# A gated mix of a long convolution and attention: x transposed half by the crossbar and half by TensorE, and another threshold for zero matmuls

## The chip, the cores and the metric

One Trainium2 chip, of which the program uses one core. A core has TensorE (matmuls, in the profile PE, its weight loads PEld), VectorE (DVE), ScalarE (ACT), GpSimd (POOL) and SyncE (SP), each working through its own list of instructions in order, and 16 DMA engines. The engines meet at semaphores. The metric is the device time of one execution in microseconds; times named here are medians of several runs, unless a profiled execution is meant.

## The reference

Two branches read the same x = A_q of shape 1 x 2048 x 640. One is a convolution: k is filtered with four taps, multiplied by v, convolved over the whole sequence with a long filter, and multiplied by x. The other is attention with 32 query heads of 20 channels that share one key head and one value head. A gate, the sigmoid of a dot product of x with gate_w, mixes them.

```python
def _B_ref(x, wq, wk, wv, wo):
    q = (x @ wq).reshape(B, S, H, Dh).transpose(0, 2, 1, 3)
    k = x @ wk
    v = x @ wv
    scores = einsum("bhqd,bkd->bhqk", q, k) * (Dh ** -0.5)
    p = softmax(scores, axis=-1)
    o = einsum("bhqk,bkd->bhqd", p, v)
    return o.transpose(0, 2, 1, 3).reshape(B, S, H * Dh) @ wo

x = A_q
g = sigmoid((x * gate_w).sum(-1, keepdims=True))
a = _A_ref(x, A_k, A_v, A_shift_k, A_ssm_k, A_ssm_D)   # q * (conv(kv, ssm_k) + kv * ssm_D)
b = _B_ref(x, B_wq, B_wk, B_wv, B_wo)
return g * a + (1 - g) * b
```

The scores of attention are 32 x 2048 x 2048, and every one of them is exponentiated. In the kernel that is the work of ScalarE (most of it) and VectorE.

## The kernel before

The kernel is written as a graph of operations, each with an engine, the operations it depends on, a rough cost and a priority. A planner (class Scheduler) then walks a clock over the five engines. On each engine it takes, of the operations that are ready by its own estimates, the one with the lowest priority number, and so fixes the order of every engine's list before the program is built. Waits on semaphores are put in from the dependencies (emit). So an edit of a priority or of an estimated latency moves instructions, and a wait stands wherever an instruction needs what another engine or a DMA made.

Two kinds of TensorE work are not in the graph. Where the planner finds nothing to do and TensorE's planned busy share over the last 2.4 us is under FILL, it puts in a matmul of zeros: in the opening from filler0 (L1486), during the stream of exponentials from filler (L1482), there only if the next score group is more than 0.1 us away.

**The opening** (up to the first exponential). x has four blocks of 512 rows, b = 0 to 3. Attention needs x transposed, xT, with channels on partitions. Blocks 0 to 2 come by DMA transpose through the crossbar, issued from SP (L722). Block 3 is loaded as it is into xn (L565) and transposed by TensorE in three groups of 8, 8 and 4 (L865), each copied from PSUM into xT by ScalarE or VectorE (copy_alts, L598 and L599; the planner picks). From xT come: kvn, one group of 20 small matmuls a block, giving k, v and the gate's dot product by rows (L907); kT, k transposed and repeated for four row groups (L893); and qp, the q projection of the first two of eight groups of heads (L949). The gate's weights reach the matmul operand wkv by one small transpose (L885) and one copy (L887), and kvn waits for it.

A bound on the scores is folded into the queries: ScalarE squares k out of kvn's PSUM bank (ksq, L913), VectorE sums (ksum, L920) and takes the maximum (kmcol, L923), a matmul spreads it (L926), three small operations make a root of it (kmaxr, kroot), and with the root of the squared queries (sq L959, q2 L965, ci L971) one operation makes the row cr (L974). A DMA from SP writes it into qT (the list crow0 holds this DMA). The first score matmuls (L1023) wait for that DMA. Many things that belong to later stages are made to wait for crow0 as well: loads of k, v and the remaining blocks of xn (load_x, which the convolution needs), second halves of the trigonometric tables on POOL (tables2), and the rest of wq.

ScalarE also makes the first part of the sine and cosine tables (L791, L794), with the Sin activation table; then an activation named warm (L798) loads the Exp table, after all the Sin operations.

**The stream.** attention() lists 767 exponentials of alternately 3 and 2 score tiles of 128 x 512 (ETA in banks 0 to 2, ETB in banks 3 and 4; L1055). Score group n+1 may start when exponential n-1 has freed its banks. DVE_J names the tiles that VectorE exponentiates with integer operations instead. Matmuls of probabilities with v (L1097) accumulate in bank 6. The convolution's spectra, products and inverse, later q projections and output projections are fitted around these by the planner, in banks 5 and 7. After the last exponential a short tail (tail) finishes the last group of heads, with TensorE, VectorE and the output DMAs.

The edit touches loads, tables, xT, load_x, kproj, qproj and the constants FILL and NX.

Of the kernel before, what the change touches and what calls it, by code (L numbers as in the profile page):

```python
# [18 lines left out]
FILL = 0.55  # L19
# [494 lines left out]
MAC_ALT = ()  # L514
SCALE = float(DH) ** -0.5
# [14 lines left out]
def c_act(n):  # L530
    return 0.18 + 0.833e-3 * n
# [10 lines left out]
class Kernel:  # L542
# [162 lines left out]
    def loads(self):  # L705
        T, aps = self.T, self.aps
        x = aps["A_q"][0].rearrange("(i p) d -> p i d", p=128)
        self.dma(T["wkv"][:, :, 0:20], aps["B_wk"].rearrange("(dc p) c -> p dc c", p=128), writes=["wk"],
                 nbytes=50000, eng="act", prio=-98.8)
        self.dma(T["wkv"][:, :, 20:40], aps["B_wv"].rearrange("(dc p) c -> p dc c", p=128), writes=["wv"],  # L710
                 nbytes=50000, eng="act", prio=-98.7)
        wq = aps["B_wq"].rearrange("(dc p) n -> p dc n", p=128)
        self.dma(T["gw5"][:, :], aps["gate_w"].rearrange("(dc p) -> dc p", p=128), writes=["gw5"], nbytes=2000,
                 eng="act", prio=-98.65)
        self.dma(T["wqst"][:, :, 0:160], wq[:, :, 0:160], writes=[("wqst", 0)], nbytes=204800, eng="act", prio=-98.6)
        xl = None
        x = aps["A_q"][0].rearrange("(i p) d -> p i d", p=128)
        self.dma(T["xn"][:, 12:16, :], x[:, 12:16, :], writes=[("xn", 3)], nbytes=655360, prio=-9)
        for b in range(NB - 1):
            o = T["xT"][:, :, 512 * b:512 * b + 512]  # L720
            i = aps["A_q"][0][512 * b:512 * b + 512, :]
            xl = self.g.add("sp", lambda e, o=o, i=i: e.dma_start_transpose(o, i), (), [("xT", b)], 0.1, kind="d",  # L722
                            nbytes=655360, prio=-8 + b, lat=1.6)
            xl.iss = 3.3

        self.xl = [xl]
        self.dma(T["wqst"][:, :, 160:640], wq[:, :, 160:640], writes=[("wqst", 1)], nbytes=614400, prio=-4,
                 after=self.xl)
        self.dma(T["Dbc"][:, :], aps["A_ssm_D"].partition_broadcast(128), writes=["Dbc"], nbytes=163840, prio=30,
                 after=self.xl)  # L730
# [39 lines left out]
    def tables(self):  # L770
# [6 lines left out]
        for c in range(H):  # L777
# [21 lines left out]
                            ["warm"], 1.5, prio=-1500.0, after=list(sins)))  # L799
        self.sins = sins  # L800
# [55 lines left out]
    def xT(self):  # L856

        T = self.T
        b = NB - 1
        for d0, nd in ((0, 2), (2, 2), (4, 1)):  # L860
            gr = self.group("xT", 1.0, banks=(0, 1, 2, 3, 4, 5, 7))
            for dc in range(d0, d0 + nd):
                for ci in range(4):
                    i = 4 * b + ci
                    self.mm(gr, lambda e, bk, i=i, dc=dc, ci=ci, d0=d0: e.transpose(  # L865
                        self.bank_bf(bk, 128, 512 * (dc - d0) + 128 * ci), T["xn"][:, i, 128 * dc:128 * dc + 128],
                        T["ident"][:, :]), [("xn", b), "ident"], 0.09)
            out = T["xT"][:, d0:d0 + nd, 512 * b:512 * b + 512]
            al = self.copy_alts(out, lambda bk, nd=nd: self.bank_bf(bk, 512 * nd).rearrange(
                "p (d t) -> p d t", d=nd), True)  # L870
            self.evac(gr, "dve", None, (), [("xT", b)], 0.45, alts=al)

    def load_x(self):
        T = self.T
        x = self.aps["A_q"][0].rearrange("(i p) d -> p i d", p=128)
        for b in range(NB - 1):
            self.dma(T["xn"][:, 4 * b:4 * b + 4, :], x[:, 4 * b:4 * b + 4, :], writes=[("xn", b)], nbytes=655360,
                     prio=30 + b, name="ld_x", after=self.crow0)

    def kproj(self):  # L880
# [8 lines left out]
        for b in range(NB):  # L889
            gr = self.group("kT", (1.16 if b == 0 else 4.0) + 0.1 * b, banks=ALLB if b == 0 else (7, 4, 5))  # L890
# [11 lines left out]
        for b in range(NB):  # L902
            gr = self.group("kvn", 1.5 + 0.1 * b, banks=ALLB)
            for ci in range(4):
                tc = 4 * b + ci
                for dc in range(NDC):
                    self.mm(gr, lambda e, bk, ci=ci, tc=tc, dc=dc: e.matmul(  # L907
                        self.bank(bk, 41, 44 * ci), T["xT"][:, dc, 128 * tc:128 * tc + 128], T["wkv"][:, dc, 0:41],
                        start=(dc == 0), stop=(dc == NDC - 1)), [("xT", b), "wk", "wv", "wg"], 0.05)

            def view(bk, lo, n=20):
                return self.bank(bk, 176).rearrange("p (t c) -> p t c", c=44)[:, :, lo:lo + n]
            self.evac(gr, "act", lambda e, bk, b=b, view=view: e.activation(  # L913
                T["ksq"][:, 4 * b:4 * b + 4, :], view(bk, 0), ACT.Square), (), [("ksq", b)], c_act(80))
# [7 lines left out]
                     name="ksum")  # L922
        self.dve(lambda e: e.tensor_reduce(T["kmcol"][:, :], T["ksum"][:, :], AX.X, ALU.max),  # L923
# [17 lines left out]
    def qproj(self, I, gs, prio, banks, ng):  # L941
# [3 lines left out]
        par = I % 2  # L945
        for gl, gi in enumerate(gs):
            gr = self.group("qp", prio, banks=banks)
            for dc in range(NDC):
# [4 lines left out]
                if dc == 0:  # L953
# [4 lines left out]
                      alts=self.copy_alts(qt[:, gi, :], lambda bk: self.bank(bk)))  # L958
            self.dve(lambda e, gi=gi, gl=gl: e.tensor_tensor(T[f"sq{gl}"][:, :], qt[:, gi, :], qt[:, gi, :],  # L959
                                                             ALU.mult),  # L960
                     [("qT", par, gi)], [("sq", gl)], c_fast(512), prio=prio - 500, port=True, name="sq")
        gr = self.group("q2", prio - 500, banks=banks)
# [7 lines left out]
        pr = -5000.0 if I == 0 and gs[0] == 0 else prio - 500  # L970
# [570 lines left out]
```

## Time and profile before

| | |
|---|---|
| median of five runs | 908.62 us (907.76 to 909.42) |
| profiled execution, its time | 908.86 us |
| profiled execution, its span | 906.8 us |
| first exponential starts | 23.65 us |
| last exponential ends | 897.44 us |
| ETA, 128 x 1536, one | 1489 ns mean, 384 of them |
| ETB, 128 x 1024, one | 1072 ns mean, 383 of them |
| zero matmuls, opening and stream | 18 and 149 weight loads |

The span is what the profile's clock covers from the first to the last instruction; a run's own time is some 2 us longer. Durations of exponentials overlap, since ScalarE starts one while the last drains, so the sum of the two means over all is more than the engine's busy time; the chain of waits counts each only from where the one before it ended. In the page's rows "idle before" is the time in which the engine stood still just ahead of such an instruction, with what ended most of it.

### The profile page before, as it was taken

Reading aid. Unit: us, or ns where it says so; the run is one execution under the profiler, and the core shown is the slowest. Engines: PE = TensorE matmul, PEld = TensorE weight load, DVE = VectorE, ACT = ScalarE, POOL = GpSimd, SP = SyncE. Lnnn points to the kernel's source line nnn. Section 1 sums busy time; section 2 is a strip of 40 time slices with the busy share of each in tenths; the row PEclk is TensorE's granted clock in tenths of the full one; section 3 lists DMA queues with packets and bytes.
Section 4 is the critical chain, followed back from the end, with each engine's and each line's share of the span. In section 5 each row is a group of like instructions: output and inputs, shape, how many; then the busy total and the mean of one; then the engine's idle time right before and its main releaser. Section 6 shows DMA issues by size and latency. Waiting matters only on the chain.

```text
span 906.8 us, 16333 instructions
## 1 busy us (share of the span) xinstructions
PE 852.0 (94%) x6950; PEld 350.4 (39%) x7013; DVE 633.0 (70%) x878; ACT 884.2 (98%) x791; POOL 380.5 (42%) x330
## 2 busy tenths in 40 slices
PE   7999999999999999999999999999999998998897
PEld 3344344443433344343333333343443332432233
DVE  6456743456766768866886678876678886787964
ACT  5999999999999999999999999999999999999995
POOL 2940056870426496153675212769125494000000
PEclk9999999999999999999999999999999999999999
DMA  7930200010000010000010200000000000301111
GB/s 163 212 128 3 65 20 20 13 31 18 20 19 14 15 35 20 19 20 17 14 32 18 56 20 13 19 8 19 20 19 19 14 7 26 89 13 35 63 35 52
DMA packets 58507, 32.69 MB, mean 36 GB/s; under 512 B 41154, under 2 KB 54466, under 8 KB 58434
## 3 DMA queue, kind: packets, MB, share of 16 engines
q1 hardware_dynamic: 56168, 31.05, 12.7%
q8 instruction: 55, 0.90, 0.4%
q10 hardware_dynamic: 2266, 0.59, 0.3%
q14 instruction: 18, 0.15, 0.1%
HBM read 18.01 MB, written 6.02 MB: 27 GB/s over the span
## 4 chain that ended last, share of the span: by engine, by line
ACT 68%; PE 24%; DMA 3%; SPq 2%; DVE 2%; issue 1%; DVEq 0%
ACT ETA L1055 41%; ACT ETB L1055 27%; PE ps L1023 7%; PE ps L1336 5%; PE ps L1097 5%; PE ps L1400 3%; PE ps L949 2%; SPq L1253 1%; DMA rbc<-scr_d 1%; DMA kTr<-in_A_k_dram 1%; DMA xT<-in_A_q_dram 1%; PE ps L1270 1%; PE ps L1434 1%; PE ps L1187 1%; SPq L722 1%
## 5 line engine op out<-in xcount | busy, mean ns | idle before, releaser
L1055 ACT ACTIVATE ETA<-ps 128x1536 bf16<-128x1536 f32 x384 | 571.7, 1489 | 3.6 <-PE ps L1097 2.3
L1055 ACT ACTIVATE ETB<-ps 128x1024 bf16<-128x1024 f32 x383 | 410.7, 1072 | 0.2 <-PE ps L1023 0.2
L1023 PE MATMUL ps<-qT,kT 21*128 21x512 bf16 x2048 | 302.5, 384 | 34.8 <-ACT ETA L1055 22.8
L1367 POOL TENSOR_TENSOR Pp<-X,K 128x512 f32<-128x512 bf16 x120 | 168.6, 1430 | 358.4 <-DVE K L1355 351.0
L1097 PE MATMUL ps<-ETA,vaug 128*32 128x512 bf16 x1150 | 196.1, 389 | 0.4 <-DVE acc L1151 0.3
L1097 PE MATMUL ps<-ETB,vaug 128*32 128x512 bf16 x766 | 188.1, 389 | 0.0
L1023 PEld LDWEIGHTS ps<-qT,kT 21*128 21x128 bf16 x2048 | 74.7, 91 | 223.6 <-ACT ETA L1055 123.2
L1085 DVE TENSOR_SCALAR dJ<-ps 128x512 uint32<-128x512 f32 x132 | 90.7, 687 | 44.0 <-PE ps L1023 43.7
L1093 DVE SCALAR_TENSOR_TENSOR ETd<-dJ,dE 128x1024 bf16<-128x1024 f32 x66 | 89.4, 1354 | 19.5 <-PE ps L1097 19.4
L1090 DVE SCALAR_TENSOR_TENSOR dE<-dJ,dE 128x1024 f32<-128x1024 uint16 x66 | 89.9, 1362 | 0.5
L1092 DVE SCALAR_TENSOR_TENSOR dJ<-dJ 128x1024 f32<-128x1024 uint16 x66 | 89.3, 1353 | 0.4
L1367 POOL TENSOR_TENSOR AB<-Pp 128x256 bf16<-128x256 f32 x80 | 77.2, 965 | 4.9
L1400 PE MATMUL ps<-AB,Tcos 128*128 128x256 bf16 x320 | 78.2, 275 | 1.1 <-DVE dJ L1085 1.0
L1097 PEld LDWEIGHTS ps<-ETA,vaug 128*32 128x32 bf16 x1150 | 47.7, 93 | 65.6 <-issue 63.0
L1400 PE MATMUL ps<-AB,Tsin 128*128 128x256 bf16 x280 | 69.3, 275 | 0.0
L1097 PEld LDWEIGHTS ps<-ETB,vaug 128*32 128x32 bf16 x766 | 45.2, 92 | 43.5 <-issue 42.9
L1367 POOL TENSOR_TENSOR Pp<-Pp 128x512 f32<-128x512 f32 x40 | 60.9, 1524 | 2.7
L1088 DVE TENSOR_SCALAR dE<-dJ 128x1024 uint32<-128x1024 uint32 x66 | 54.1, 820 | 0.5
L1336 PE MATMUL ps<-ssm_kT,Tsin 128*128 128x256 bf16 x320 | 53.7, 275 | 0.0
L1336 PE MATMUL ps<-kv,Tsin 128*128 128x256 bf16 x320 | 53.7, 275 | 0.0
L1336 PE MATMUL ps<-kv,Tcos 128*128 128x256 bf16 x320 | 52.0, 275 | 1.2 <-DVE kv L1410 0.5
L1336 PE MATMUL ps<-ssm_kT,Tcos 128*128 128x256 bf16 x320 | 51.8, 275 | 0.4 <-DVE dJ L1085 0.3
(135 smaller groups left out, 807.2 us busy)
## 6 DMA issues: line engine op xcount, KB each, us to landing
rbc<-scr_d SPq DMA_DIRECT2D x31, 256.0 KB
scr_o<-oTn SPq DMA_DIRECT2D x24, 128.0 KB, 1.7
xn<-in_A_q_dram SPq DMA_DIRECT2D x4, 640.0 KB
kv<-in_A_v_dram SPq DMA_DIRECT2D x4, 640.0 KB, 5.1
out_dram<-outsb SPq DMA_DIRECT2D x14, 160.0 KB, 1.8
oTp<-scr_o SPq DMA_DIRECT2D x12, 160.0 KB, 5.2
wog<-in_B_wo_dram SPq DMA_DIRECT2D x4, 200.0 KB
wo<-in_B_wo_dram SPq DMA_DIRECT2D x4, 200.0 KB, 3.4
```

Source lines behind the costliest of these rows:

```text
L949: o = self.mm(gr, lambda e, bk, gi=gi, dc=dc: e.matmul(self.bank(bk), T["wq_pad"][:, dc, 128 * gi:128 * gi + 128], T["xT"][:, dc, 512 * I: ...
L1023: return e.matmul(self.bank(bk), T["kT4"][32 * r:32 * r + 21, 128 * j:128 * j + 128], T[f"qT{G // 8 % 2}"][32 * r:32 * r + 21, G % 8, :], ...
L1055: op("act", lambda e: e.activation(et(n)[:, 0:w], self.ps[:, lo:lo + w], ACT.Exp, scale=SCALE), [("ps", base[n % 2] + k) for k in range(le ...
L1085: self.evac(gr, "dve", lambda e, bk, h=h: e.tensor_scalar(J[:, 512 * h:512 * h + 512], self.bank(bk), SCALE * LOG2E * 65536.0, EOFF * 6553 ...
L1088: V(lambda e: e.tensor_scalar(E[:, :], J[:, :], 7, 0x7F800000, ALU.logical_shift_left, ALU.bitwise_and), [kJ], ["dE"], c_fast(1024), **k)
L1090: V(lambda e: e.scalar_tensor_tensor(Ef, lo, ED, Ef, ALU.add, ALU.mult), [kJ, "dE"], ["dE"], c_ps(1024), **k)
L1092: V(lambda e: e.scalar_tensor_tensor(Jf, lo, EP, lo, ALU.add, ALU.mult), [kJ], [kJ], c_ps(1024), **k)
L1093: V(lambda e: e.scalar_tensor_tensor(T["ETd"][:, :], Jf, EQ, Ef, ALU.add, ALU.mult), [kJ, "dE"], ["ETd"], c_ps(1024), **k)
L1097: return op("pe", lambda e: e.matmul(self.bank(6)[32 * r:32 * r + 32, :], T["vaug"][:, j, :], src, start=(j == 0), stop=(j == NSC - 1), ti ...
L1336: o = self.mm(gr, lambda e, bk, lhs=lhs, rhs=rhs, comp=comp, n=n: e.matmul(self.bank(bk, 256, 256 * comp), lhs, rhs, start=(n == 0), stop= ...
L1367: f = lambda e: e.tensor_tensor(out, a, b, alu)
L1400: self.mm(gr, lambda e, bk, lhs=lhs, fc=fc, comp=comp, h=h: e.matmul(self.bank(bk, 256, 256 * h), lhs, AB[:, fc, :, comp, :], start=(fc == ...
```

## The change

Five things are edited.

- **x.** NX = 2: blocks 0 and 1 come by crossbar transposes, blocks 2 and 3 are loaded into xn and transposed by TensorE, so 40 transposes in six groups instead of 20 in three. The copies out of PSUM get a high priority. load_x, after crow0, brings two blocks of xn instead of three.
- **Gate weights.** Their load moves to the head of ScalarE's DMA queue, with a longer estimated latency.
- **kT of block 0** gets a later priority (1.95 instead of 1.16), behind the kvn groups of lower number.
- **Squares and the bound.** ksq, the first q copies, their squares and q2 get high priorities, and the activation that loads the Exp table now depends on all four ksq.
- **FILL** goes from 0.55 to 0.62.

```diff
-FILL = 0.55
+FILL = 0.62
...
+NX = 2
...
         self.dma(T["gw5"][:, :], aps["gate_w"].rearrange("(dc p) -> dc p", p=128), writes=["gw5"], nbytes=2000,
-                 eng="act", prio=-98.65)
+                 eng="act", prio=-98.9, lat=6.2)
...
-        self.dma(T["xn"][:, 12:16, :], x[:, 12:16, :], writes=[("xn", 3)], nbytes=655360, prio=-9)
-        for b in range(NB - 1):
+        for b in range(NX, NB):
+            self.dma(T["xn"][:, 4 * b:4 * b + 4, :], x[:, 4 * b:4 * b + 4, :], writes=[("xn", b)], nbytes=655360,
+                     prio=-9)
+        for b in range(NX):
             o = T["xT"][:, :, 512 * b:512 * b + 512]
...
-            xl.iss = 3.3
+            xl.iss = 4.8 if b == 0 else 3.3
...
+        self.warm = sins[-1]
...
-        b = NB - 1
-        for d0, nd in ((0, 2), (2, 2), (4, 1)):
-            gr = self.group("xT", 1.0, banks=(0, 1, 2, 3, 4, 5, 7))
+        for b, d0, nd in [(b, d0, nd) for b in range(NX, NB) for d0, nd in ((0, 2), (2, 2), (4, 1))]:
+            gr = self.group("xT", 1.0 + 0.01 * b, banks=(0, 1, 2, 3, 4, 5, 7))
...
-            self.evac(gr, "dve", None, (), [("xT", b)], 0.45, alts=al)
+            self.evac(gr, "dve", None, (), [("xT", b)], 0.45, alts=al, prio=-2000.0)
...
-        for b in range(NB - 1):
+        for b in range(NX):
             self.dma(T["xn"][:, 4 * b:4 * b + 4, :], x[:, 4 * b:4 * b + 4, :], writes=[("xn", b)], nbytes=655360,
                      prio=30 + b, name="ld_x", after=self.crow0)
...
-            gr = self.group("kT", (1.16 if b == 0 else 4.0) + 0.1 * b, banks=ALLB if b == 0 else (7, 4, 5))
+            gr = self.group("kT", (1.95 if b == 0 else 4.0) + 0.1 * b, banks=ALLB if b == 0 else (7, 4, 5))
...
-                        start=(dc == 0), stop=(dc == NDC - 1)), [("xT", b), "wk", "wv", "wg"], 0.05)
+                        start=(dc == 0), stop=(dc == NDC - 1)), [("xT", b), "wk", "wv", "wg"], 0.03)
...
-                T["ksq"][:, 4 * b:4 * b + 4, :], view(bk, 0), ACT.Square), (), [("ksq", b)], c_act(80))
+                T["ksq"][:, 4 * b:4 * b + 4, :], view(bk, 0), ACT.Square), (), [("ksq", b)], c_act(80), prio=-4500.0)
...
+        self.warm.deps.update(self.g.writer[("ksq", b)] for b in range(NB))
...
+        first = I == 0 and gs[0] == 0
...
-                      alts=self.copy_alts(qt[:, gi, :], lambda bk: self.bank(bk)))
+                      alts=self.copy_alts(qt[:, gi, :], lambda bk: self.bank(bk)), prio=-2500.0 if first else None)
...
-                     [("qT", par, gi)], [("sq", gl)], c_fast(512), prio=prio - 500, port=True, name="sq")
-        gr = self.group("q2", prio - 500, banks=banks)
+                     [("qT", par, gi)], [("sq", gl)], c_fast(512), prio=-5500.0 if first else prio - 500, port=True, name="sq")
+        gr = self.group("q2", -5500.0 if first else prio - 500, banks=banks)
```

What the planner makes of it, in the changed program's lists up to the first score. SP: two plain loads of xn, two crossbar transposes, then as before. TensorE: ten zero matmuls, 40 transposes, the gate's transpose, kvn of blocks 0 and 2, kT of block 0, the q projection, kvn of blocks 1 and 3, four zero matmuls, q2, two more, the spread of the maximum, kT of blocks 1 to 3, two more, scores. ScalarE: one table pair, copies of xT among further table parts, two ksq, the last short xT copy, Tcos, q copy, Tsin, q copy, ksq, Tcos, ksq, the copy of kT's block 0, the Exp table, the other three copies of kT, the first exponential. VectorE takes the second xT copy of each of the two blocks. In the stream the list has 194 zero matmuls.

More of the change, by code (lines that the diff above doesn't have):

```diff
@@ L969, in qproj @@
         ci, cr = T["ci"], T["cr"]
-        pr = -5000.0 if I == 0 and gs[0] == 0 else prio - 500
+        pr = -5000.0 if first else prio - 500
         self.evac(gr, "dve", lambda e, bk: e.tensor_scalar(
```

## The prediction

> **What bounds the kernel now.** I read the page first, then ScalarE's waits, then the chain of waits at both ends, then the timeline of the opening.
>
> ```profile
> PE 852.0 (94%) x6950; PEld 350.4 (39%) x7013; DVE 633.0 (70%) x878; ACT 884.2 (98%) x791; POOL 380.5 (42%) x330
> ...
> PEclk9999999999999999999999999999999999999999
> ```
>
> ScalarE is busy 98% of the span, and TensorE was granted its full clock in every slice. ScalarE's waits over the whole span (waited for: us, times, longest):
>
> ```profile
> ACT L775 <- issue: 3.3, 1, 3.3
> ACT kT L900 <- PE ps L893: 2.9, 2, 2.5
> ACT ETA L1055 <- PE ps L1097: 2.3, 6, 1.1
> ```
>
> The exponentials (ETA, ETB) waited 2.3 us here, and by two further lines 0.8 (the very first) and 0.2. The chain near the end shows the pace (start, us, what):
>
> ```profile
> 889.18 0.92 ACT ETB L1055
> 890.09 1.42 ACT ETA L1055
> 891.51 0.92 ACT ETB L1055
> 892.43 1.34 ACT ETA L1055
> ```
>
> There are 767 exponentials: 383 pairs of 1.34 and 0.92 and one short one of 0.66, together 866.2 us. The first starts at 23.65, the last ends at 897.44: 873.8 us, so 7.6 us are lost in the whole stream. From there to the span's end are 9.4 us. Span = 23.65 + 873.8 + 9.4 = 906.8; the run took 908.86, so 2.06 lie around the span. The change can win in the first term, which is set by this part of the chain:
>
> ```profile
> 12.83 2.10 PE ps L949 x9
> 14.93 1.08 PE ps L893 x5
> 16.01 0.22 PE ps L907 x9
> 16.23 0.67 ACT kT L900
> ...
> 16.92 1.28 ACT L798
> ...
> 18.41 0.13 ACT ksq L913
> ...
> 18.56 0.38 DVE ksum L920 x2
> 18.94 0.58 DVE ci L971
> ...
> 20.61 0.45 DVE cr L974
> ...
> 21.09 1.85 DMA qT<-cr
> ```
>
> The reader is to see that the activation-table load (1.28) stands ahead of the last two squares of k (ksq), on which the key maximum, the offset row cr and its DMA into qT wait. The last xT block is not the tight point: it lands at 14.47 (the wqst load that waits for it issues at 14.48), while TensorE is busy with L949 and L893 until 16.0.
>
> **The change, part by part.** Times below are worked out with rows of this trace, in the order in which the changed program's instructions stand on each engine.
>
> *Loads.* SP now issues two plain x loads and two crossbar transposes, not one and three. A plain 655 KB load at the 268 GB/s of 2.5 to 5.0 us takes 2.4 us, about what one transpose takes (by the semaphores of the trace the three landed at 7.36, 12.05 and 14.47; the last two are 2.4 apart). So the second x block lands near 5.7 + 2.4 = 8.1, xT block 0 near 7.36 + 2.4 = 9.8 and block 1 near 14.4. By the order they are wanted at 8.7, 10.5 and 15.1: covered by 0.6 to 0.7 us each; a later landing than that costs its excess. The gate vector moves ahead of wk and wv on ScalarE's queue; the four issues still end at 3.3, and wk's copies on POOL are wanted only at 11.85. wqst and Dbc still issue after the last transpose. Cost: nothing, under the cover named.
>
> *Transposes on TensorE.* Before (start, us, operation):
>
> ```profile
> 6.68 1.28 PE L865 MATMUL ps<-ident,xn 128*128 128x128 bf16 x20
> 7.33 1.02 ACT L599 ACTIVATE xT<-ps 128x1024 bf16<-128x1024 bf16 x1 [1.26 <-PE ps L865]
> ```
>
> Now there are 40, and ten zero matmuls ahead of them instead of nine (nine took 3.88: 0.43 each cold; warm ones are 0.22 apart; I take 0.3, a little on the slow side). ScalarE's first copy thus begins at 7.63 and ends at 8.65. The next copy of 1024 goes to VectorE, which the trace does not show. Nearest row: VectorE's copy of 512 from PSUM, 0.68; at the same rate 1024 take 1.23. The Trainium skill ("VectorE: DVE Perf Modes", the perf-mode tier table) says that a copy from PSUM reaches twice the rate if all is 16-bit with unit step: as an estimate 0.69. By the row the start of the stream is 0.54 later than by the rule. Both tensors here are bf16, the row's source is float32, so I take 0.69: 8.7 to 9.4. ScalarE's short copy (0.59) ends at 10.05; the gate transpose waits for it, then VectorE's copy into wkv (0.16 + 0.18 and handovers): the first kvn group starts at 10.5, and all of TensorE's opening stands behind it.
>
> *TensorE from 10.5.* kvn block 0 to 11.2, block 2 to 11.85 (20 took 0.67), kT 1.08 to 12.93, ten q projections at 0.216 to 15.09, kvn blocks 1 and 3 (40 took 1.17) to 16.26. This is what sets the path; before, the same kvn pair ended at 17.02.
>
> *Squares ahead of the table load.* ksq gets priority and the Exp load waits for all four. On ScalarE: second q copy 15.27 to 15.87, ksq 1, Tcos (0.72), ksq 3 ends at 16.9, against 18.54 before. The table load is not saved: it now waits for ksq 3 and the first kT copy, runs 17.45 to 18.73 beside the VectorE chain, and has three kT copies queued behind it. VectorE: ksum, gsum, kmcol to 17.4, ci to 18.0, kmaxr 0.28, kroot, kmaxr and two vaug copies (0.19 each) between them, cr ends at 19.4 (the link took 2.53 from ksq to cr before and takes 2.5 now). The row's DMA 1.85, TensorE's wake and three scores take what they took before (21.07 to 23.65: 2.58), so from cr's end at 19.35 to 19.4 the **first exponential starts at 21.95**, 1.7 earlier.
>
> *What is late next.* All three remaining kT copies now stand on ScalarE before the first exponential; before, the third was on VectorE. The last kT matmuls wait for the first of these copies (18.95 to 19.64): they run 19.85 to 20.93, the copy 21.13 to 21.82. It ends some 0.1 before; so any further gain on the row would stop there.
>
> *More zero matmuls.* The stream's go from 149 to 194, 45 × 0.213 = 9.6 us more TensorE work. Their price is bounded by: below, 0 or a small gain if the clock were at risk; above, 45 × 0.12, the part of 0.22 that exceeds the 0.1 gap in which they are allowed, 5.4 us. A score group takes 0.4 and has an exponential of 0.92 to 1.34 to hide under, so I take 0. The clock gives nothing back: "TensorE: Matmul & The Clock Gate" (HAM oscillation) asks only that no pause exceed some 3.4 us, and the longest pause between weight loads after 6.4 us, up to the tail, was 1.93 us (at 10.15). By the row and by the rule alike, fills past 0.55 raise no clock.
>
> *The rest.* Two late x loads instead of three after the row, POOL's table copies and later orders shift; none ends a wait of ScalarE in 23.65 to 896. Exponentials, VectorE exponentials and tail (L1211, L1218, L1233) stand as before: 0, with the 7.6 us lost in the stream likely to fall otherwise by some 1.2 either way, as its single largest wait is 1.1.
>
> Sum: 908.86 − 1.7 = 907.16 for the profiled run, which lay 0.24 over the median of the five; against the median 908.62, **906.9**.
>
> **Rivals.**
>
> 1. *The gain is hidden anyway.* VectorE's copy at the row's 1.23 takes 0.54, a transpose that lands 0.6 past its cover as much again. For it: covers under 1 us on a queue whose landings were uneven. Against: bf16 on both sides. It takes both to leave a gain of some 0.6: 908.0.
>
> 2. *Zero matmuls in the scores' way (the other side).* Place: the stream after 500 us, where 110 of the before's 149 stand. Price: up to 5.4 us; it decides once 14 of the 45 cost 0.12 (1.7 us). At half of it, 2.7, the time is 909.6; at all of it 912.3. For it: TensorE is 94% busy and in order. Against: with 149 of them ScalarE's waits for TensorE in the stream were 2.5 us in all.
>
> 3. *The clock falls in the opening.* From 7.0 to 10.5 TensorE has only transposes and the tiny gate. The same page (Part 4) says that transposes do not count as busy for the clock. If so, the pause is 3.5 us, just over its window, and the work of 10.5 to 16.26 starts at half rate: in the trace cold zero matmuls took 0.43 against 0.22 warm, and weight loads fell from 147 to 98 ns only 3.7 us after the first one. Half of 3.7 is 1.85 later, twice that if the clock returns a window late: 908.8 to 910.6. By the row (20 transposes and a pause to 8.5, no drop) it costs nothing. I take the row, because 40 transposes fill over half of that stretch.
>
> **How the numbers follow.** Forecast 0.72 (own range 905.2 to 908.6: start ±0.7, stream ±1.2), rival 1 0.11, rival 2 0.10, rival 3 0.07. About 0.2% (1.8 us) is what a measurement of this kernel can tell from no change; the border of faster is 906.8, close to the forecast. Where I had a choice in the opening (the tenth fill, Tcos ahead of ksq 3, handovers) I took the slow value, so of the forecast's 0.72 somewhat more than half is faster, 0.45, 0.25 the same and 0.02 slower. Rival 1 is the same with 0.10, rival 2 slower with 0.09, rival 3 slower with 0.05; the small rest is the same but for 0.01. That makes 0.45, 0.38, 0.17. The range 905.2 to 909.7 takes in rival 2 at its half, and leaves out its upper half and the clock's second window.
>
> **What would show it.** First exponential near 21.95 (from 23.65), ksq's last end before the table load, VectorE's xT copy near 0.69, kvn's last pair ending near 16.3, third kT copy on ScalarE just ahead of the first score; from the first to the last exponential 873.8 again; tail 9.4. Wrong if the first exponential is later than 23, if pieces of a cold clock (zero matmuls or projections 0.43 apart) appear after 8 us, or if ScalarE's waits for TensorE in the stream grow by over 1.5 us.

## The result, and the profile after

| | before | changed |
|---|---|---|
| median of the runs compared | 909.64 us (907.57 to 913.39, 71 runs) | 911.41 us (909.58 to 919.08, 36 runs) |
| profiled execution, its time and its span | 908.86, 906.8 us | 910.40, 908.6 us |
| first exponential starts | 23.65 us | 22.70 us |
| last exponential ends | 897.44 us | 899.29 us |
| between the two | 873.8 us | 876.6 us |
| zero matmuls in the stream | 149 | 194 |

The ratio is 1.0029, with an interval of 1.0020 to 1.0038: **slower by 1.8 us**, where 1.7 less was forecast (906.9, against the 908.62 of the first five runs). The runs of both kernels scatter with the clock that TensorE was granted (a run's mean clock is given as a share of full speed). Of the changed kernel's runs the 16 whose mean clock was 0.999 or 1.000 have a median of 910.6; its five at 0.993 took 915.3 to 916.0. The kernel before was measured again with each of the four series of experiments below, and its runs at 0.999 or more have medians of 908.1 to 908.8 there. So the gap between the kernels is about as large at full clock (1.8 to 2.4) as over all runs, and the two profiles, both at full clock, can be compared. Numbers from different series are good to some 0.7 us.

The page of the changed kernel, engine rows and clock row:

```profile
PE 863.8 (95%) x7010; PEld 357.4 (39%) x7078; DVE 638.9 (70%) x878; ACT 886.0 (98%) x794; POOL 388.2 (43%) x330
...
PEclk9999999999999999999999999999999999999999
```

ScalarE is still the bound and the clock is whole; TensorE has 11.8 us more work. ScalarE's waits over the span (waited for: us in total, times, longest):

```profile
ACT ETA L1061 <- PE ps L1103: 4.7, 10, 1.9
...
ACT ETA L1061 <- PE ps L1029: 0.3, 1, 0.3
ACT ETB L1061 <- PE ps L1029: 0.2, 1, 0.2
```

The first row was 2.3 us in six waits before. All waits of the stream together went from 2.5 to 5.2 us, about as much as the time between the first and the last exponential grew (2.8). I then lined up the ends of the 767 exponentials of both profiles (changed minus before, worked out from the traces):

| exponential | 0 | 32 | 192 | 480 | 640 | 672 | 766 |
|---|---|---|---|---|---|---|---|
| time before, us | 25.1 | 61.6 | 244.4 | 572.6 | 754.1 | 791.4 | 897.4 |
| difference, us | -0.96 | +0.10 | +1.50 | +0.41 | +0.95 | +1.83 | +1.85 |

The start is earlier by one microsecond, not 1.7, and **that gain is gone by 62 us**. Further on the difference moves both ways; its largest single steps are at 791 us (+0.84), 235 us (+0.83) and 609 us (+0.62).

**The opening.** TensorE's timeline in the changed kernel (start, us, operation; in brackets the idle time before it and what ended that):

```profile
7.21 1.45 PE L869 MATMUL ps<-ident,xn 128*128 128x128 bf16 x20
9.19 1.28 PE L869 MATMUL ps<-ident,xn 128*128 128x128 bf16 x20 [0.53 <-ACT xT L601]
10.54 0.16 PE L889 MATMUL ps<-ident,gw 5*128 5x5 bf16 x1
10.98 1.18 PE L911 MATMUL ps<-wkv,xT 128*128 128x41 bf16 x40 [0.28 <-DVE wkv L891]
...
15.24 1.17 PE L911 MATMUL ps<-wkv,xT 128*128 128x41 bf16 x40
16.26 1.02 PE L1492 MATMUL ps<-ident,zeros 128*128 128x512 bf16 x4
17.21 0.59 PE L971 MATMUL ps<-sq,IndG 128*8 128x512 bf16 x2
...
21.68 0.59 PE L1492 MATMUL ps<-ident,zeros 128*128 128x512 bf16 x2
22.21 0.80 PE L1029 MATMUL ps<-qT,kT 21*128 21x512 bf16 x5
```

kvn starts at 10.98 (10.5 forecast), and zero matmuls stand ahead of q2 at 17.21, whose squares were ready near 16.5, and ahead of the first scores at 22.21. VectorE's timeline:

```profile
9.08 0.69 DVE L600 COPY xT<-ps 128x1024 bf16<-128x1024 bf16 x1 [2.76 <-ACT xT L601]
...
17.84 0.68 DVE L977 TENSOR_SCALAR ci<-ps 8x512 int32<-8x512 int32 x1 [0.27 <-PE ps L971]
...
19.29 0.47 DVE L980 TENSOR_SCALAR cr<-ci,kmaxr 8x512 bf16<-8x512 f32 x1
```

The copy of 1024 took 0.69, as the rule of the Trainium skill gave it ("VectorE: DVE Perf Modes", the perf-mode tier table). The bound's row cr ends at 19.76, 0.36 after the forecast.

**The stretch to 62 us.** TensorE, then ScalarE, of the changed kernel:

```profile
33.57 0.34 PE L1276 MATMUL ps<-kdiag,kTr 128*128 128x128 bf16 x3
34.74 0.49 PE L1276 MATMUL ps<-kdiag,kTr 128*128 128x128 bf16 x6 [0.84 <-DVE kv L1280]
35.17 0.39 PE L1029 MATMUL ps<-qT,kT 21*128 21x512 bf16 x2
```

```profile
35.63 1.02 ACT L1061 ACTIVATE ETB<-ps 128x1024 bf16<-128x1024 f32 x1 [0.18 <-PE ps L1029]
36.98 1.45 ACT L1061 ACTIVATE ETA<-ps 128x1536 bf16<-128x1536 f32 x1 [0.33 <-PE ps L1029]
```

TensorE stands 0.84 us ahead of a group of the convolution of k (L1276), the scores queued behind it come late, and ScalarE waits. The view names VectorE, whose copy out of PSUM ends at 34.64. But the group needs block 1 of kTr as well, and by its semaphore that landed at 34.61. Which of the two it was can be seen in experiment 10, with the changed kernel's own list on TensorE, and in the kernel before: the matmuls of both groups run in one piece there, the second group starting before VectorE's copy has even begun. In the kernel before:

```profile
34.56 0.62 PE L1270 MATMUL ps<-kdiag,kTr 128*128 128x128 bf16 x8
34.88 0.69 DVE L1274 TENSOR_TENSOR kv<-ps,kv 128x512 bf16<-128x512 f32 x1 [3.57 <-PE ps L1270]
```

Block 1 had landed at 34.30 there, 0.4 us before it was wanted. In the changed kernel it is wanted at 33.8. The transfers on SP's queue did move up with the row, the second as much as the first. The transpose of block 1 is issued like this, before and then changed:

```profile
27.49 4.77 SPq L1253 DMA_TRANSPOSE kTr<-in_A_k_dram  x1
26.16 4.87 SPq L1259 DMA_TRANSPOSE kTr<-in_A_k_dram  x1
```

Block 0 landed at 27.48 instead of 28.82. A transfer of this kind raises its semaphore sixteen times. For block 1, fifteen of these had come by 33.04, early enough, and only the sixteenth came at 34.61. Beside this, from 32.38 to 33.50, the trace has one DMA packet of 16 KB of the kind "instruction" (by its name, a piece of the program itself), and the transfer's last two small packets end at 33.51 and 33.52, just behind it. The profiles of experiments 4 and 7 have the same picture: such a packet until 33.89 and 33.32, fifteen by 33.37 and 32.87, and the sixteenth at 34.95 and 34.44. In the kernel before no 16 KB packet of that kind lies between 14.9 and 38.5, and all sixteen came within 0.14 us. So it looks as if the last part of the block stood behind a load of program code. No run moved that load, so this is read from three traces and not tested.

### The profile page after: what moved, and what is told of

The parts are those of the page before. It is cut to its first block, busy times and chain, and to the rows that moved or that the text cites. A ratio compares the mean times of both kernels' runs of the same rounds, so it can differ in the third digit from the quotient of the medians.

```text
span 908.6 us, 16446 instructions
## 1 busy us (share of the span) xinstructions
PE 863.8 (95%) x7010; PEld 357.4 (39%) x7078; DVE 638.9 (70%) x878; ACT 886.0 (98%) x794; POOL 388.2 (43%) x330
## 4 chain that ended last, share of the span: by engine, by line
ACT 62%; PE 34%; DVE 2%; DMA 1%; issue 0%; SPq 0%; DVEq 0%; POOL 0%; POOLq 0%
ACT ETA L1061 38%; ACT ETB L1061 24%; PE ps L1029 9%; PE ps L1342 7%; PE ps L1103 6%; PE ps L955 3%; PE ps L1406 3%; PE ps L1276 1%; DMA rbc<-scr_d 1%; PE ps L1492 1%; DVE ETd L1099 1%; PE ps L1440 1%; PE ps L971 0%; DMA wo<-in_B_wo_dram 0%; PE ps L1193 0%
## 5 line engine op out<-in xcount | busy, mean ns | idle before, releaser
L1373 POOL TENSOR_TENSOR Pp<-X,K 128x512 f32<-128x512 bf16 x120 | 171.8, 1456 | 336.4 <-DVE K L1361 310.9
L1098 DVE SCALAR_TENSOR_TENSOR dJ<-dJ 128x1024 f32<-128x1024 uint16 x66 | 87.1, 1320 | 0.3
L1094 DVE TENSOR_SCALAR dE<-dJ 128x1024 uint32<-128x1024 uint32 x66 | 58.2, 882 | 0.4
L1342 PE MATMUL ps<-kv,Tsin 128*128 128x256 bf16 x320 | 51.6, 275 | 0.0
```

The lines of the kernel that those rows point to most:

```text
L1094: V(lambda e: e.tensor_scalar(E[:, :], J[:, :], 7, 0x7F800000, ALU.logical_shift_left, ALU.bitwise_and), [kJ], ["dE"], c_fast(1024), **k)
L1098: V(lambda e: e.scalar_tensor_tensor(Jf, lo, EP, lo, ALU.add, ALU.mult), [kJ], [kJ], c_ps(1024), **k)
L1342: o = self.mm(gr, lambda e, bk, lhs=lhs, rhs=rhs, comp=comp, n=n: e.matmul(self.bank(bk, 256, 256 * comp), lhs, rhs, start=(n == 0), stop= ...
L1373: f = lambda e: e.tensor_tensor(out, a, b, alu)
```

## The experiments

Three theories. **Z**: the added zero matmuls stand in the scores' way. **O**: the moved opening and the order that the planner makes of it lose the time. **C**: the granted clock decides. Times at "full clock" are medians of the runs whose mean clock was 0.999 or more. "Not issued" and "moved" mean that TensorE's or SP's finished list was edited, so that nothing else was planned anew.

**1 and 2. The threshold alone, in either kernel.**

```diff
-FILL = 0.55
+FILL = 0.62
```

> The kernel before with FILL at 0.62 alone. Theory Z (zero matmuls stand in the way, in the opening and in the stream): slower than before by 1.5 to 2.5 us (ratio 1.002 to 1.003), first exponential some 0.8 later than 23.65 because two more zero matmuls stand ahead of the key maximum and two ahead of the first scores, and first to last exponential some 875 to 876 instead of 873.8. Theory O (the moved opening and the order that the planner makes from it cost the time): same as before within 1 us. Theory C (the granted clock: half-clock stretches decide): fewer runs below a clock of 0.998 than the kernel before and so not slower.

Measured: 915.56 us (910.75 to 926.91), ratio 1.0063 (1.0039 to 1.0087); no run above a clock of 0.995. In its profile the clock was at half from 12.75 to 16.16 and from 634.0 to 640.8, and the first exponential starts at 25.52. C expected the clock to be held better, and it was held worse. The other way round, the changed kernel with 0.55:

```diff
-FILL = 0.62
+FILL = 0.55
```

> The changed kernel with FILL back at 0.55: the opening change alone. Theory Z: faster than the kernel before by about 1 us (ratio 0.999), since the opening's gain stays. Theory O: slower by 1.5 to 3 us, like the whole change, the start some 1 us earlier and the stream some 2.5 us longer. Theory C: as slow or slower than the whole change, with at least as many runs under a clock of 0.998.

Measured: 931.07 us (930.81 to 933.19), ratio 1.0242 (1.0226 to 1.0257), clock 0.962 to 0.967. Its clock row on the page:

```profile
PEclk9999999999999999999999999589999975999999
```

The clock was at half from 584.0 to 611.3 and from 754.7 to 792.2, and for 3.4 us at 48.1. The digits 5, 8 and 7, 5 are the two long stretches. Either threshold can lose the clock, since a new threshold also makes a new order; the changed kernel's gain or loss can't be read from the threshold alone.

**3. The stream's zero matmuls not issued**, the changed kernel's own order otherwise.

```diff
+        gone = [o for o in sch.order["pe"] if o.name == "fill" and o.fn is sch.filler]
+        sch.order["pe"] = [o for o in sch.order["pe"] if o not in gone]
```

> The changed kernel in its own order, but the 194 zero matmuls of the stream are not issued (they add nothing to any result). Theory Z: first to last exponential shorter than the 876.6 of the change by 1.5 us or more, time near or under the kernel before. Theory O: first to last exponential as in the change within 0.7 us. Theory C: more runs with a granted clock under 0.998, down to 0.98, and a median over that of the change by several us; weight loads or score groups at half pace in the thin stretches after 500 us.

Measured: 987.57 us (981.18 to 995.07), ratio 1.0855 (1.0809 to 1.0901), clock 0.863 to 0.879:

```profile
PEclk9799999899999999999787896688799655977599
```

The 194 zero matmuls hold up a clock that is worth 77 us. Z can't be tested by removal.

**4. The eight late zero matmuls of the opening not issued** (those after the first ten).

```diff
+        gone = [o for o in sch.order["pe"] if o.name == "fill" and o.fn is sch.filler0][10:]
```

> The changed kernel in its own order, but the eight zero matmuls of the opening that come after the q projections (four ahead of q2, two ahead of the key maximum's matmul, two ahead of the first scores) are not issued. Theory Z: first exponential at 22.0 to 22.2 instead of 22.70. If in addition the earlier start is given back before 62 us, because TensorE there works on k as it lands, the last exponential ends no earlier than in the change and the time is the same within 0.5 us; if it is kept, 0.6 us faster than the change. Theory O expects nothing of it: start 22.7.

Measured: 912.54 us (908.15 to 925.24), ratio 1.0010 (0.9992 to 1.0029). In its profile the first exponential is 0.56 us earlier than in the changed kernel, so these eight did stand in the way. (Counted from the start of kvn it is 10.87 us instead of 11.72, so they cost 0.85; kvn itself started later in this execution.) But now TensorE waited longer for kTr:

```profile
33.01 0.34 PE L1276 MATMUL ps<-kdiag,kTr 128*128 128x128 bf16 x3
35.08 0.50 PE L1276 MATMUL ps<-kdiag,kTr 128*128 128x128 bf16 x6 [1.74 <-DMA kTr<-in_A_k_dram]
35.51 0.39 PE L1029 MATMUL ps<-qT,kT 21*128 21x512 bf16 x2
35.83 0.61 PE L1103 MATMUL ps<-ETA,vaug 128*32 128x512 bf16 x3
```

Here the view names the transfer. After the pause the matmul goes from 0.39 to 0.61: the clock was at half from 35.8 to 42.6, and from the first exponential to the 33rd this profile lost 3.8 us more than the changed kernel's, the longer wait included. At full clock this version takes 908.3, against 908.8 for the kernel before in this series. These are only five of its 22 runs, though, and perhaps the ones in which kTr came in time and so no pause cost the clock; none of them was profiled.

**5. Every zero matmul of the stream issued twice.**

```diff
+            twice.append(o)
+            if o.name == "fill" and o.fn is sch.filler:
+                f = Op("pe", sch.filler, c_mm(512), "c", "fill", 0.0)
...
+                twice.append(f)
```

> Changed kernel's own order, every zero matmul of the stream issued twice: 388 instead of 194, nothing else moved. Z (zero matmuls stand in the scores' way): if the 1.8 us are the price of the 45 added ones, that is 0.04 us each, and 194 more cost about 7.8 us: near 919. C (the granted clock decides): the clock is held at least as well, mean clock 0.998 or more in most runs, and a zero matmul ahead of a waiting score group is nearly free: 909.5 to 912. O (the new order itself loses the time at full clock): same as the changed kernel at full clock, 910 to 911.5.

Measured: 932.15 us (931.87 to 932.91), ratio 1.0249 (1.0229 to 1.0268), clock 0.999 in every run. ScalarE's waits:

```profile
ACT ETA L1061 <- PE ps L1103: 12.1, 31, 1.2
ACT ETA L1061 <- PE ps L1029: 7.1, 18, 0.7
```

All three numbers are missed, C's and O's by 20 us and Z's by 13. At full clock a second zero matmul in the same gap costs on average 21.6 / 194 = 0.11 us. So the price exists. Whether the 45 of the change pay it is the next question.

**6. The same number added where there is room.** The kernel before, with one zero matmul more ahead of each of the 45 score groups after 480 us ahead of which TensorE stood longest.

```diff
+        for o in todo:
+            f = Op("pe", sch.filler, c_mm(512), "c", "fill", 0.0)
...
+            pe.insert(pe.index(o), f)
```

> Kernel before in its own planned order with 45 more zero matmuls in the stream, as many as the change adds, one each ahead of the 45 score groups after 480 us ahead of which TensorE stood longest in the profile (0.3 to 0.9 us); nothing else moved. Z (each costs what the second copies cost in the doubled run, 21.6 us over 194, 0.11 us): 5 us, near 914.4. C and O (a zero matmul that fits the standing time of TensorE is free, and the clock of the kernel before is at most a little better held): 908.5 to 909.5, and ScalarE's waits at those places do not grow.

Measured: 909.09 us (907.52 to 922.14) against 909.43, ratio 0.9993 (0.9983 to 1.0003). ScalarE's waits there:

```profile
ACT ETA L1056 <- PE ps L1098: 2.2, 7, 0.7
```

They were 2.3 us in six. The upper end of the interval leaves 0.3 us for all 45. A zero matmul that fits the standing time is free, one that doesn't costs 0.11 on average: Z holds only for the second kind. These 45 stand where there was room. The change's own 45 were not taken out of its list; what is known of them comes from ScalarE's waits, further down.

**7 and 8. Zero matmuls put by hand where TensorE stood.** In the version of experiment 4, seven ahead of the waiting group of k's convolution and five near 792 us:

```diff
+EXTRA = [(244, 7), (6247, 5)]
```

> Changed kernel's own order without the 8 late zero matmuls of the opening (whose median was 912.5 with a clock of 0.996 in half its runs, and 908.2 in its runs at 0.998 or more), and with 7 zero matmuls put just ahead of the k-convolution group that waited 1.74 us for its block of kTr at 33.3, and 5 ahead of the inverse-transform matmul that waited 1.2 us near 792. C: the half-clock windows from 35.8 to 42.6 go, mean clock 0.998 or more in most runs, median 908 to 909.5. Z: twelve more zero matmuls cost up to 0.2 us each, 912.5 to 915. O: the clock is a side effect, median stays near 912.5.

Measured: 910.28 us (909.58 to 911.78), ratio 1.0009 (1.0000 to 1.0018), no run under a clock of 0.998. The half clock is gone, as C said; but the version is not down to the 908 to 909.5 expected, for the wait on kTr is still there, now filled with zeros:

```profile
33.41 1.67 PE L1489 MATMUL ps<-Tcos,zeros 128*128 128x512 bf16 x7
34.92 0.50 PE L1277 MATMUL ps<-kdiag,kTr 128*128 128x128 bf16 x6
```

The same was tried on experiment 1, at some 18 places:

```diff
+EXTRA = [(56, 6), (4622, 2), (4629, 1), (4632, 4), (5046, 1), (5048, 3),
...
```

> Kernel before with the threshold 0.62 in its own planned order (median 915.6, clock 0.975 to 0.995), plus 6 zero matmuls ahead of the second group of kvn in the opening, where TensorE waited 2.3 us for a block of xT, and 1 to 4 zero matmuls at about 18 places of the stream (578-580, 633-640, 715-719, 742-745, 848-849 us) where TensorE stood for 0.35 to 1.1 us in thin windows. C: of the 2.62 us by which its last exponential stood behind the kernel before's, 1.9 come from a half-clock window in the opening and 2.5 from two at 634-641; with them gone it is ahead by up to 1.7: median 906.5 to 908.5 with clock 0.998 or more. Z: more zero matmuls only add, 915.6 or more. O: its order is the loss, 911 or more at full clock.

Measured: 917.52 us (913.29 to 929.68), ratio 1.0082 (1.0048 to 1.0116), clock 0.973 to 0.993. The half clock of the opening is gone, and the first exponential starts at 23.70 instead of 25.52. For the rest it is a miss: the profile still has half clock at 580.2, 634.9 and 720.2. The places were read off one execution and the added work was too little; how much would have been enough was not tried.

**9. The first block of k ahead of the row's DMA.**

```diff
+        k0.deps.difference_update(self.crow0)
+        for q in (sch.order["sp"], sch.linear):
+            q.remove(k0)
+            q.insert(q.index(row), k0)
```

> Changed kernel's own order with one DMA moved: the first transpose of k is issued ahead of the row's DMA, once the tables are made (about 16.5 instead of 22.1), so that the second block of kTr lands near 31 instead of 34.6. O, in the form that the start gain is held up by kTr's landing: the stretch from the first exponential to the 33rd takes 36.5 us as in the kernel before and not 37.6, TensorE's wait of 0.84 at 34.7 goes, the time falls by 0.7 to 1.1 (about 910.4), unless the row's DMA lands later for the transfer ahead of it, by up to 1 us, which would show at the first exponential. Z and C: no change beyond the clock's scatter, 911.4.

Measured: 912.13 us (908.83 to 916.76), ratio 1.0030 (1.0014 to 1.0046), 909.5 at full clock in only three runs. Both halves of O's expectation came true and cancelled. The first exponential came 0.93 later, since the row's DMA lay behind the transfer, and the stretch to the 33rd took 36.6 us and not 37.6, for TensorE no longer waited at 34.7. The median does not tell them apart.

**10. The first block of v ahead of the row's DMA instead**, which leaves the two transposes of k next to each other.

```diff
+        v0.deps.difference_update(self.crow0)
+        for q in (sch.order["sp"], sch.linear):
+            q.remove(v0)
+            q.insert(q.index(row), v0)
```

> Changed kernel's own order with one DMA moved: the first block of v is issued ahead of the row's DMA, at about 13 us, when SP and the queues stand idle, instead of between the first two transposes of k. The second block of kTr then lands near 31 instead of 34.6, and the row's DMA has nothing ahead of it. O (the start gain is held up by kTr's landing): first exponential at 22.7 as in the changed kernel, the stretch from the first exponential to the 33rd takes 36.5 instead of 37.6, so 0.9 to 1.0 less: 909.5 at full clock, 910 to 910.7 in the median. Z and C: as the changed kernel, 911.4 with 910.5 at full clock. If v's block collides with the wqst load, the q projections and so the first exponential come later.

Measured: 909.28 us (907.78 to 918.72), ratio 1.0011 (0.9998 to 1.0025); 908.9 at full clock, **1.7 under the changed kernel's 910.6**, which is of another series; above the kernel before of its own series it is 0.5. SP's queue, then TensorE:

```profile
13.91 0.43 SPq L567 DMA_DIRECT2D kv<-in_A_v_dram  x1
19.40 0.73 SPq L567 DMA_DIRECT2D qT<-cr  x1
...
21.70 6.62 SPq L1259 DMA_TRANSPOSE kTr<-in_A_k_dram  x2
```

```profile
33.19 0.68 PE L1277 MATMUL ps<-kdiag,kTr 128*128 128x128 bf16 x9
33.80 0.39 PE L1029 MATMUL ps<-qT,kT 21*128 21x512 bf16 x2
```

The nine matmuls that stood on both sides of the 0.84 us run in one piece; block 1 of kTr landed at 30.35. From the first exponential to the 33rd the time falls by 0.98 against the changed kernel's profile, more than the 0.84 of the wait and less than the 1.06 that the stretch had lost. A further 1.24 fell at 791 us, which I had not expected. The first exponential starts at 22.32 here, but not through the move, whose transfer issues only at 13.91: in this execution the clock was whole from 5.65 on and not from 7.55, kvn started 0.37 earlier, and from there it is the same 11.7 us. This execution was also the fastest of the 22, so the two profiles differ by 2.6 us where the medians differ by 1.7.

**11. Both repairs together**: experiment 10's move in experiment 7's version, with two zero matmuls instead of seven ahead of the group that no longer waits.

```diff
-EXTRA = [(244, 7), (6247, 5)]
+EXTRA = [(244, 2), (6247, 5)]
```

> The same move of v's first block in the guarded version (without the 8 late zero matmuls of the opening, with 2 zero matmuls ahead of the k convolution that had waited, and 5 near 792). O and C together: first exponential near 22.1 to 22.3, the 33rd 1.2 to 1.6 earlier than in the guarded version, clock 0.998 or more: 908.7 to 909.2 in the median, which is level with the kernel before. C alone: 910.3 as the guarded version. Z: no difference from the guarded version beyond five zero matmuls fewer, 909.7 to 910.3.

Measured: 908.64 us (908.14 to 909.73), clock 0.998 or more in all 22 runs, **ratio 0.9989 (0.9981 to 0.9997)**: under the changed kernel by 2.8 us and, barely, under the kernel before in its series (909.43). At full clock it is level with it, 908.6 against 908.4. Its median is the lower one because its clock scatters less.

**12. TensorE's list mended at three places** of that version, where ScalarE waited 0.73, 0.54 and 1.07 us for an exponential's buffer.

```diff
+        new = list(R(1936)) + [*R(1949, 1953), *R(1945, 1949), *R(1936, 1945)]
+        new += list(R(1953, 4870)) + [*R(4875, 4881), *R(4870, 4875)]
...
```

> The guarded version with v's first block early, and TensorE's list mended at three places where ScalarE waited 0.73, 0.54 and 1.07 us for matmuls of probabilities with v that had to free an exponential's buffer: at 235 and 609 us these matmuls (and at 235 the scores) go ahead of a burst of transform matmuls, at 790 they and the scores go ahead of inverse-transform matmuls that wait for VectorE, with 3 zero matmuls in place of 5. O (the planner's order of the changed kernel loses time at such places at full clock): 1.5 to 2.3 us less than the 908.64 of the version it starts from, 906.3 to 907.2, below the kernel before. If the place in the list is not the cause (the waits come back behind the burst, or at VectorE), no change: 908.3 to 909. C and Z expect no change, 908.6.

Measured: 908.69 us (908.10 to 918.64), ratio 0.9995 (0.9983 to 1.0007), 908.5 at full clock. A miss. ScalarE near the third place, in the new version:

```profile
798.57 1.45 ACT L1062 ACTIVATE ETA<-ps 128x1536 bf16<-128x1536 f32 x1
800.80 1.02 ACT L1062 ACTIVATE ETB<-ps 128x1024 bf16<-128x1024 f32 x1 [0.78 <-PE ps L1030]
802.25 1.45 ACT L1062 ACTIVATE ETA<-ps 128x1536 bf16<-128x1536 f32 x1 [0.42 <-PE ps L1030]
```

The marked exponential no longer waits; the next two do, behind the burst that was put off. Only at 609 us did some 0.4 us stay won. (This profile is of the slowest of the 15 runs. At 235 us it had half a clock for 3.4 us, so its waits there can't be read, and again from 555.0 to 575.5.)

## Why the prediction was wrong

**The step that failed** is the one called "The rest": late loads, table copies and orders shift, "none ends a wait of ScalarE in 23.65 to 896", and so the stream stays at 873.8. It took 876.6. I had counted the DMAs of the moved opening and the queue ahead of the row, but not what stands behind the row on SP: four transposes of k and four blocks of v, in turn. The order of TensorE's list put k's convolution earlier with the earlier start; the last part of kTr's second block did not come earlier (34.61 against 34.30). Experiments 9 and 10 show it by two different moves: with that block there in time, the stretch to the 33rd exponential takes 36.6 us instead of 37.6 (36.5 before), so it keeps what the opening won. It is rival 1's "hidden anyway" in kind, but at a place that I had not looked at. Why the last part came late is less sure: it was not the order of the queue, which moved up, and the code packet beside it is not tested. That the orders of the stream "shift" for nothing failed too; see the sum below.

**The start** (21.95 forecast, 22.70 measured). The mechanism was right: the squares end before the table load, and the row comes earlier. Sizes were off by 0.75 in all. The ten zero matmuls ran cold for longer than I took them to, and ScalarE's first copy came at 8.02, not 7.63; kvn was at 10.98, not 10.5. cr ended at 19.76, not 19.4; the third copy of kT on ScalarE ended at 22.58, not 21.82. The zero matmuls of the opening after the tenth had no term at all in my sum. From the start of kvn to the first exponential it is 11.7 us in the profiles that have them (this one, experiments 5 and 10) and 10.8 to 10.9 in those that have not (4, 7, 11 and 12), where I had 11.45. So kvn cost 0.5 more than my sum, these zero matmuls 0.85, and the rest of it 0.6 less: in part the errors cancelled. VectorE's copy, weighed by row and rule, was right at 0.69.

**Zero matmuls.** "I take 0" is right for those that find room (experiment 6), and the upper end of 0.12 is about what they cost where there is none (0.11, experiment 5). The prediction's own sign came true: ScalarE's waits for TensorE in the stream grew by 2.7 us, over the 1.5 named. But they are twelve waits and not a loss spread over the list, and the three long ones (at 235, 609 and 791 us) have no zero matmul in TensorE's timeline near them. So rival 2 did not decide, though its price was real.

**"Fills past 0.55 raise no clock" did not hold.** With 0.55 the changed program ran at a clock of 0.965, 20 us slower than with 0.62. But experiment 2 also plans the order anew, and in the kernel before 0.62 lowered the clock (experiment 1), so the threshold alone does not decide. I took the Trainium skill's condition on pauses, some 3.4 us ("TensorE: Matmul & The Clock Gate", HAM oscillation), for the whole condition. In experiment 1 the clock fell in the opening after a standing time of 2.3 us, and at 634 us where no two weight loads were over 1.1 us apart. So a long pause is not needed.

**Rival 3** did not happen: the changed profile's clock is whole from 7.55 us on. From there to 10.5 TensorE has transposes alone, save for the gate's small one at the end, and kvn at 10.98 runs at full clock.

**Of the 1.85 us** by which the last exponential is late, -0.96 is the start, +1.06 the stretch to 62 us (0.98 of it shown to hang on kTr's landing), +0.85 lies between 62 and 754 us, and +0.90 behind that, nearly all of it the step at 791.

The +0.85 is the new order of the stream (whether the moved opening or the threshold made the planner choose it was not separated). The profiles of experiments 4, 7, 9, 10 and 11 keep that order but for a few zero matmuls, and show 0.87 to 0.91 between the same two exponentials. It is a sum of gains and losses. Its two largest losses, and then the step at 791, stand in ScalarE's timeline of the changed kernel as

```profile
235.46 1.45 ACT L1061 ACTIVATE ETA<-ps 128x1536 bf16<-128x1536 f32 x1 [0.73 <-PE ps L1103]
608.49 1.45 ACT L1061 ACTIVATE ETA<-ps 128x1536 bf16<-128x1536 f32 x1 [0.54 <-PE ps L1103]
791.83 1.45 ACT L1061 ACTIVATE ETA<-ps 128x1536 bf16<-128x1536 f32 x1 [1.90 <-PE ps L1103]
```

The first two come back in experiments 10 and 11 with the same 0.73 and 0.54; at 235 and 609 us the kernel before has no wait. The matmuls that ScalarE waits for stand behind a burst of transform matmuls there. The step at 791, where TensorE stood 1.81 us for VectorE, is another matter: in the six profiles of this order it lies between -0.42 and +0.84, so it is mostly the single execution's. Moving instructions at the three places did not win the time back (experiment 12): how much of it another order could win stays open. The clock's half-speed stretches explain the scatter of the runs, and not the gap of the medians.

## What to carry to other kernels

When an edit brings a phase forward, follow the queue that is released at its end: list what stands behind the last transfer, and ask of each block whether all of it comes earlier by as much, since a wait ends with the last part. A filler instruction is free while it fits the standing time of an in-order engine and costs its excess beyond it, so put it ahead of a wait that the profile shows and do not go by a share of busy time alone; and judge such fillers at equal granted clock, since the clock and the price pull opposite ways. A planner that lays out the whole program anew for one changed constant makes a new program: edit its finished list when one cause is to be measured.

## What the runs showed that was not expected

The granted clock changes in steps of 3.41 us: spans at half clock in these profiles last from 3.41 to 64.85 us (the longest in experiment 3), all multiples of it but for the one that the program's end cuts off, and at half clock a matmul of 512 columns goes from 0.39 to 0.61 us. I found no sharp limit. An estimate of TensorE's share of each such step, over all 14 profiles, counts a matmul of 512 columns as 0.213 us, the spacing of two at full clock, times the part of the array that its rows and columns take. By it the clock fell after steps with shares from 0.17 to 0.44 and stayed after 102 others with 0.30 to 0.44, so this share alone does not decide. One lost step lowers a run's mean clock by 3.41 / 2 / 907 = 0.0019. In the changed kernel the runs at 0.993 took 5.2 us more than those at 0.999 and above, so 0.006 to 0.007 of clock or 3.2 to 3.7 steps: about 1.5 us for each. In experiment 4 two steps cost 3.8 us, with the longer wait for kTr in them. Since executions of one program differ in where their steps fall, a program with thin stretches scatters by several microseconds although nothing in it changes.
